# A new stored order for all pieces of an attention and feed-forward kernel

## The chip, the cores and the metric

One core of one Trainium2 chip runs the whole program. The metric is the device time of one execution in microseconds (us). Engines are named as in the profile: PE (TensorE), PEld (its weight loads), DVE (VectorE), ACT (ScalarE), POOL (GpSimd) and SP (SyncE, which only issues transfers). "Clock" is the share of full speed that PE was granted.

## The reference, cut to what matters

Forgetting attention over 8 batches and 8 heads of 576 rows by 64, then an RMS norm and a gated feed-forward part over the 4608 rows of 512:

```python
decay = cum[:, :, :, None] - cum[:, :, None, :]        # cum = cumsum(log f)
scores = where(causal, -1e9, scale * q @ k.T + decay)
attn = exp(scores - max); attn = attn / (sum(attn) + 1e-9)
x = (attn @ v)  # heads side by side: 4608 x 512
xn = x / sqrt(mean(x * x) + 1e-6) * rms_g              # 512 weights
g = xn @ w_gate; out = (g * sigmoid(g) * (xn @ w_val)) @ w_out      # 512 -> 1536 -> 512
```

Inputs and output are fp32; the kernel multiplies in bf16.

## The kernel before

The kernel is a list of some 1,500 pieces of work (load, cast, transpose, scores, exp, mask, values, norm, gate, projection, store). Each piece belongs to one engine, and each engine runs its own in order. A string, ORDER, gives the order of all of them; semaphores follow from what each piece reads and writes.

```python
ORDER = """
one lf ident Lk0.0 Lq0.1 rg identb clear Lk0.1 Lq0.0 ... clip turn_rg*48 ...     # *48: that many filler matmuls first
...
"""
```

Names that the argument needs: `L`, `C` and `Sv` load, cast and scale the inputs of a batch (`Ck3.0`: cast of k of batch 3, part 0; casts and scalings mostly on POOL), `msc` and `mask` apply the causal mask (POOL), `xn1.2` is the norm of block 2 of batch 1 (DVE), `xtr1.2` its transposes (PE), `pj`, `o` and `so` project a block, copy it out of PSUM and store it (PE, ACT, POOL), `g` and `v` are the gate and value matmuls.

```python
def norm(js, j):                                        # DVE, 40 times
    xn = T["xn", b, j] = xnp.tile([128, DM], BF16, name="xn", tag="xn")
    nc.vector.scalar_tensor_tensor(xn, in0=T["x", b][:, j, :], scalar=T["rs", b, js][:, j:j + 1], in1=rgb,
                                   op0=ALU.mult, op1=ALU.mult)
...
def store(j, c0, c1):                                   # the last group's from SP, all 32 others from POOL
    (nc.sync if end else nc.gpsimd).dma_start(out=out[t0 + j * 128:t0 + (j + 1) * 128, c0:c1],
                                              in_=T.pop(("o", g, j, c0))[:, 0:c1 - c0])
```

`rgb` is the RMS weight spread over all 128 partitions. Three `ores` buffers hold rows on their way out; a store gives its buffer back when it has landed.

The softmax here doesn't subtract the row's maximum and nothing guards it: scores larger than these inputs give would overflow.

Of the kernel before, what the change touches and what calls it, by code (L numbers as in the profile page):

```python
# [11 lines left out]
ACT = mybir.ActivationFunctionType  # L12
# [10 lines left out]
one lf ident Lk0.0 Lq0.1 rg identb clear Lk0.1 Lq0.0 Lq0.2 Lqk11 Lk0.2 clip turn_rg*48 keep_rgT Lqk00 Ck0.0 fetch_ln spread_rg*3 Lv0.0 Cq0.1 log scan  # L23
Lv0.1 Cq0.0 Ck0.1 tr0.01*29 tr0.00 Cq0.2 Lk0.3 keeptr0.00.k keeptr0.00.q keeptr0.01.k expo Lqk01 keeptr0.01.q tr0.02*7 sc0.1.0 keeptr0.02.q Lv0.40
esc0.1.0 twice keeptr0.02.k Lq0.3 Ck0.2 sc0.2.0*5 msc0.1.0 turn_dec esc0.2.0 Lv0.3 sc0.0.0 tr0.03 keep_rg msc0.2.0 keeptr0.03.k Lk1.0 keeptr0.03.q
Lv0.41 keep_dec sc0.3.0*8 wv0 tr0.10 esc0.3.0 Sv0.1 Lq1.0 wg1 esc0.0.0 Ck0.3 Lv1.40 Sv0.0 fetch msc0.0.0 Lv0.2 keeptr0.10.q val0.2.0*16 Lk1.2 xpo0.2.0
msc0.3.0 val0.0.0:ff*5 sc0.1.512 xpo0.0.0 val0.4.0 esc0.1.512 Cqk0 xpo0.4.0 val0.6.0:ff Cq0.3 xpo0.6.0 Lq1.2 Ck1.0 tr0.12*8 Lk1.1 sq0.1 sc0.0.512 wg0
Lq1.3 keeptr0.12.q keeptr0.10.k trt0 sq0.0 keeptrt0 sc0.3.512*1 esc0.3.512 ms0.0 rs0.0 keeptr0.12.k sc0.2.512*10 wv1 xn0.0 esc0.2.512 Sv0.3 wg2
sc0.1.1024*10 k4.0 xn0.1 Lq1.1 xtr0.0 esc0.1.1024 Lqk10 tri esc0.0.512 kxtr0.0 Lv1.41 xtr0.1*9 Sv0.2 sc0.2.1024 Cq1.0 kxtr0.1 sc4.0 Sv0.4 esc0.2.1024
Lk1.3 g0.0*1 msc0.1.1024 Lv1.0 sc0.0.1024 th0.0 v0.0f exp4.0 ga0.0 esc0.0.1024 sc0.0.384 g0.2 mask4.0 hga0.0 esc0.0.384 msc0.0.1024 sc0.1.384 tr1.0  # L30
esc0.1.384 sc0.2.384 wv2 val0.3.2 keeptr1.0.k keeptr1.0.q sc0.3.1024 th0.2 Cq1.2 val0.1.2:ff msc0.2.1024 esc0.2.384 v0.2f Lv1.2 xpo0.1.2 esc0.3.1024
xpo0.3.2 val0.0.2:ff ga0.2 val0.4.2 msc0.3.1024 sc0.3.384 xpo0.0.2 val0.2.2:ff esc0.3.384 wg3 hga0.2 sc1.0.0 esc1.0.0 xpo0.4.2 val0.5.2:ff Lv1.3 Cq1.1
val0.7.2:ff xpo0.2.2 val0.6.2 Cqk1 xpo0.7.2 xpo0.5.2 Ck1.2 trt1*2 g0.4 xpo0.6.2 Ck1.1 keeptrt1 sq0.3 Cq1.3 tr1.1 sq0.2 tr1.2 k4.1 keeptr1.1.q
keeptr1.1.k wv3 keeptr1.2.q sc4.1*2 sq0.4 Ck1.3 th0.4 ms0.2 tr1.3*8 Lv1.1 rs0.2 keeptr1.2.k ga0.4 esc1.0.512 wo0 xn0.3 v0.4f*4 xn0.2 keeptr1.3.k wo1
g0.6 exp4.1 Lk2.0 hga0.4 sc1.0.1024 keeptr1.3.q th0.6 xtr0.3 Lq2.3 v0.6f ga0.6 kxtr0.3 xn0.4 esc1.1.0 xtr0.2 Lqk20 g0.8 kxtr0.2 hga0.6 g1.0 th0.8
esc1.0.1024 ga0.8 v1.0f Sv1.0 Lk2.1 th1.0 sc1.1.512 ga1.0 g1.2 esc1.1.1024 Lq2.0 hga1.0 v0.8f th1.2 esc1.1.512 Lk2.3 ga1.2 g0.10 hga0.8 v1.2f
msc1.1.1024 th0.10 ga0.10 sc1.2.0 mask4.1 esc1.2.0 xtr0.4 g1.4 Sv1.4 kxtr0.4 hga1.2 esc1.2.512 v1.4f th1.4 msc1.0.1024 Lq2.1 v0.10f ga1.4 Sv1.2
sc1.2.1024 hga1.4 g1.6 esc1.3.0 hga0.10 Sv1.3 v1.6f th1.6 esc1.2.1024 ga1.6 g1.8 Lqk21 Sv1.1 v1.8f th1.8 ga1.8 sc1.3.512 esc1.3.512 val1.0.0 hga1.6
Lk2.2 val1.1.0:ff hga1.8 esc1.3.1024 g1.10 pj0.0.0 msc1.3.1024 th1.10 ga1.10 msc1.2.1024 Lv2.3 xpo1.1.0 Lv2.41 xpo1.0.0 val1.2.0:ff Ck2.0 val1.4.0:ff
xpo1.2.0 Lv3.41 pj0.0.0e Cq2.0 xpo1.4.0 val1.5.0 o0.0.0 val1.3.0:ff Ck2.1 Lq2.2 xpo1.5.0 val1.6.0:ff Ck2.3 Lk3.0 xpo1.3.0 tr2.0 Cq2.1 val1.7.0 Lqk31  # L40
xpo1.6.0 keeptr2.0.k Cqk2 tr2.1 Lk3.3 keeptr2.0.q pj0.1.0 Cq2.3 keeptr2.1.k Lq3.3 xpo1.7.0 keeptr2.1.q sq1.1 Lv2.40 Sv2.3 sq1.2 Lq3.0 pj0.1.0e so0.0.0
v1.10f o0.1.0 Ck2.2 Lq3.1 sq1.4 trt2 sc2.0.0 keeptrt2 sq1.0 Cq2.2 hga1.10 tr2.3 Lqk30 sq1.3 k4.2 tr2.2 pj1.0.0 Lv2.0 ms1.0 keeptr2.2.k keeptr2.2.q
rs1.0 esc2.0.512 keeptr2.3.q Lq3.2 keeptr2.3.k xn1.3 sc4.2 pj1.0.0e xn1.0 exp4.2 xtr1.3 o1.0.0 pj1.1.0 xn1.1 kxtr1.3 xn1.2 esc2.0.0 xn1.4 xtr1.0
xtr1.1 kxtr1.0 pj1.1.0e kxtr1.1 xtr1.2 sc2.0.1024 kxtr1.2 Cq3.0 esc2.0.1024 xtr1.4 g2.0 kxtr1.4 tq3.0 o1.1.0 Cq3.1 v2.0f th2.0 Cqk3 esc2.1.0 Lv2.1
ga2.0 g2.1 Cq3.3 tq3.1 hga2.0 Ck3.3 v2.1f th2.1 Ck3.0 ga2.1 sc2.1.512 Lv2.2 mask4.2 esc2.1.512 g2.2 hga2.1 Lq4.3 msc2.0.1024 v2.2f tk3.0 th2.2 Sv2.0
esc2.1.1024 ga2.2 g2.3 Lk4.0 hga2.2 Cq3.2 v2.3f th2.3 Lk3.1 Sv2.1 ga2.3 sc2.2.0 tt3 g2.4 esc2.2.512 hga2.3 Sv2.2 tq3.2 v2.4f th2.4 Sv2.4 esc2.2.0
ga2.4 g2.5 Lq4.1 v2.5f tq3.3 th2.5 msc2.1.1024 ga2.5 val2.1.0 sc2.2.1024 Ck3.1 hga2.4 esc2.2.1024 g2.6 xpo2.1.0 Lk3.2 hga2.5 v2.6f msc2.2.1024 th2.6
tk3.1 esc2.3.0 ga2.6 val2.0.0 k4.3 val2.2.0:ff tk3.3 hga2.6 sc2.3.512 xpo2.2.0 g2.7 esc2.3.1024 xpo2.0.0 Lv3.3 val2.4.0:ff th2.7 Lqk40 sc4.3 v2.7f
xpo2.4.0 esc2.3.512 Lv3.2 ga2.7 val2.5.0 exp4.3 Lv3.0 msc2.3.1024 g2.8 hga2.7 Lv3.40 xpo2.5.0 sc3.0.0 mask4.3 Lq4.0 esc3.0.0 val2.6.0:ff Ck3.2
val2.3.0 xpo2.6.0 Cq4.3 tk3.2 th2.8 v2.8f Ck4.0 xpo2.3.0 g2.9 ga2.8 val2.7.0 hga2.8 th2.9 v2.9f Sv3.2 xpo2.7.0 esc3.0.512 tq4.3 ga2.9 g2.10 sq2.4  # L50
Sv3.3 hga2.9 v2.10f Lv3.1 sq2.3 so1.1.0 th2.10 tk4.0 g2.11 sq2.1 Sv3.0 ga2.10 sc3.0.1024 sq2.0 Lqk41 hga2.10 v2.11f Sv3.4 th2.11 Lk4.3 sq2.2 ga2.11
pj2.0.0 Lk4.1 esc3.0.1024 ms2.0 hga2.11 Cq4.0 esc3.1.0 so0.1.0 tq4.0 rs2.0 pj2.0.0e sc3.1.512 o2.0.0 Lk4.2 msc3.0.1024 pj2.1.0 xn2.1 esc3.1.1024
esc3.1.512 xn2.0 tx2.1.3 xn2.4 pj2.1.0e sc3.2.0 xn2.2 esc3.2.0 Lv4.3 pj2.2.0 Ck4.1 Lv5.41 esc3.2.512 so2.0.0 tx2.0.3 Sv3.1 pj2.2.0e tx2.2.3 sc3.2.1024
so1.0.0 esc3.2.1024 pj2.3.0 msc3.1.1024 Lq4.2 o2.1.0 esc3.3.0 Cq4.1 Lv5.40 Ck4.3 Lqk51 o2.2.0 val3.1.0 msc3.2.1024 Lk5.3 val3.3.0:ff xpo3.1.0
val3.0.0:ff tk4.1 Cqk4 sc3.3.512 xpo3.0.0 val3.5.0 esc3.3.1024 xpo3.3.0 pj2.3.0e val3.2.0:ff Cq4.2 xpo3.5.0 o2.3.0 g3.0 esc3.3.512 xpo3.2.0 tq4.1
v3.0f xn2.3 th3.0 msc3.3.1024 g3.1 ga3.0 Lq5.3 val3.4.0 so2.3.0 tk4.3 hga3.0 th3.1 v3.1f Ck4.2 ga3.1 Ck5.3 val3.7.0:ff tq4.2 xpo3.4.0 g3.2 xpo3.7.0
val3.6.0 hga3.1 Lqk50 th3.2 v3.2f Lv4.0 ga3.2 g3.3 Lk5.0 xpo3.6.0 hga3.2 tx2.4.4 v3.3f th3.3 sq3.2 ga3.3 g3.4 tt4 hga3.3 v3.4f th3.4 Sv4.0 sq3.1 Lq5.2
ga3.4 sc4.0.0 g3.5 Lq5.0 esc4.0.512 hga3.4 Lq5.1 v3.5f th3.5 Lv4.1 sq3.4 ga3.5 g3.6 k4.4 esc4.0.0 tk4.2 hga3.5 Ck5.0 v3.6f th3.6 Sv5.4 g3.7 ga3.6
sc4.2.0 th3.7 hga3.6 so2.2.0 v3.7f sq3.3 ga3.7 Sv4.3 tk5.0 esc4.2.512 g3.8 hga3.7 Cqk5 v3.8f th3.8 tx2.3.4 sq3.0 ga3.8 sc4.4 g3.9 esc4.2.0 Lv4.41
hga3.8 v3.9f Lk5.2 ms3.0 exp4.4 th3.9 mask4.4 sc4.0.1024 Lv4.40 esc4.0.1024 ga3.9 g3.10 Sv4.1 Lv4.2 hga3.9 esc4.1.0 v3.10f Cq5.0 g3.11 th3.10 rs3.0  # L60
tq5.0 ga3.10 sc4.1.512 Cq5.3 esc4.1.512 v3.11f hga3.10 Lv5.0 so2.1.0 xn3.0 tt5 th3.11 pj3.0.0 Cq5.2 ga3.11 Sv4.4 Lq6.3 hga3.11 Lqk71 xn3.1 pj3.0.0e
Lk5.1 Sv4.2 pj3.1.0 o3.0.0 xn3.2 tx3.0.4 esc4.1.1024 so3.0.0 Ck5.2 tx3.2.4 pj3.1.0e pj3.2.0 msc4.1.1024 tx3.1.4 Lv5.1 pj3.2.0e sc4.2.1024 o3.2.0 Lv6.1
val4.2.0 esc4.2.1024 tq5.2 pj3.3.0 xpo4.2.0 esc4.3.0 msc4.2.1024 o3.1.0 Ck5.1 Lq6.0 val4.3.0 msc4.0.1024 pj3.3.0e Lv5.3 xpo4.3.0 g4.0 o3.3.0 k4.5
Lv6.41 xn3.3 sc4.3.512 th4.0 Sv5.1 tq5.3 val4.4.0 esc4.3.1024 ga4.0 v4.0f xpo4.4.0 tk5.3 val4.5.0:ff Cq5.1 hga4.0 g4.1 so3.2.0 xpo4.5.0 tq5.1 Sv5.0
val4.1.0 th4.1 v4.1f ga4.1 Cq6.3 g4.2 so3.1.0 hga4.1 tk5.1 Sv5.3 v4.2f xpo4.1.0 th4.2 esc4.3.512 ga4.2 tk5.2 sc4.5 g4.3 so3.3.0 exp4.5 hga4.2
msc4.3.1024 v4.3f th4.3 Lqk61 ga4.3 g4.4 Lq6.2 hga4.3 Lqk60 val4.0.0 th4.4 val4.6.0:ff tx3.2.5 xpo4.0.0 v4.4f ga4.4 sc5.0.0 Lk6.1 xpo4.6.0 esc5.0.0
g4.5 hga4.4 Lq6.1 esc5.0.512 v4.5f Lk6.0 Cqk6 g4.6 th4.5 tt6 ga4.5 sc5.0.1024 th4.6 v4.6f esc5.1.0 ga4.6 Lq7.0 val4.7.0 hga4.5 tx3.3.5 g4.7 hga4.6
xpo4.7.0 v4.7f th4.7 Lv5.2 Ck6.0 sq4.3 ga4.7 Cq6.0 g4.8 tk6.0 esc5.0.1024 xn3.4 v4.8f hga4.7 th4.8 msc5.0.1024 sc5.1.512 sq4.0 Lv7.1 ga4.8 g4.9 Lk6.2
# [108 lines left out]
def kernel(  # L177
# [16 lines left out]
    def pool(name, bufs, **kw):  # L194
# [10 lines left out]
    plan = Plan({"st": N_ST, "ld": N_LD, "pt": N_PT, "x": 2, "xn": N_XN, "xT": 3, "hT": 2, "th": 3, "ga": 2,  # L205
                 "ores": 3, "sc": 2, "po": 1, "ff": 3})
# [705 lines left out]
```

## Time and profile before

| | before |
|---|---|
| time, median of 4 runs | 383.8 us (383.36 to 384.61) |
| span of the profiled run, mean clock | 382.2 us, 0.995 |
| PE busy | 366.8 us, 96% |
| POOL busy | 171.5 us, 45% |
| the 40 norms on DVE, summed one by one | 35.1 us, the longest 1.83 us |

PE is the bound nearly everywhere, so idle PE is what an order can change: length of a window less PE busy in it.

```profile
L688 DVE SCALAR_TENSOR_TENSOR xn<-x,rs,rgb 128x512 bf16<-128x512 f32 x40 | 33.9, 877 | 5.4 <-POOL rs L684 5.3
```

A line of the groups view has busy us of the group, mean ns of one, idle time before them and what ended it. Forty norms at a mean of 877 ns; alone, one takes 740 to 750.

### The profile page before, as it was taken

The page shows a single profiled execution, that of the slowest core. Times are in us where ns is not written, and L with a number is a line of the kernel's source. Part 1 is how long each engine was busy: PE and PEld are TensorE (multiplying, and loading weights), DVE is VectorE, ACT ScalarE, POOL GpSimd, SP SyncE. Part 2 cuts the span into 40 slices and gives each one's busy share as a digit, 9 for nine tenths or more (in the row PEclk, how much of TensorE's full clock was granted, in tenths as well). Part 3 has the DMA queues.
Part 4 walks back from the last instruction along what each step waited for, and adds up shares of the span by engine and source line. Part 5 has one row for each costly group of instructions (what it writes and reads, how often), then busy time and mean ns, then how long its engine had stood idle before and what let it go on. Part 6 is the DMA issues. An engine that isn't in the chain of part 4 may idle for free.

```text
span 382.2 us, 8426 instructions
## 1 busy us (share of the span) xinstructions
PE 366.8 (96%) x3270; PEld 203.7 (53%) x3314; DVE 243.5 (64%) x460; ACT 215.1 (56%) x357; POOL 171.5 (45%) x281
## 2 busy tenths in 40 slices
PE   8768899989999999999999999999999999999996
PEld 8646787744554644454445544554444544444443
DVE  4676875776774776467855877487348845743750
ACT  2676786578687568356655496556554353313322
POOL 4485626878397546792673359224111221001000
PEclk9899999999999999999999999999999999999999
DMA  8999996799859998999987964830001224022002
GB/s 204 212 262 234 228 234 143 166 210 175 175 118 241 188 182 177 206 198 164 219 176 133 200 149 100 119 106 14 14 30 21 84 69 98 1 63 83 0 5 108
DMA packets 144840, 52.62 MB, mean 138 GB/s; under 512 B 128220, under 2 KB 142304, under 8 KB 144800
## 3 DMA queue, kind: packets, MB, share of 16 engines
q1 hardware_dynamic: 136336, 38.82, 52.8%
q0 software_dynamic: 8384, 13.11, 14.9%
q8 instruction: 26, 0.43, 0.5%
q14 instruction: 14, 0.11, 0.1%
q10 hardware_dynamic: 80, 0.15, 0.1%
HBM read 37.90 MB, written 9.44 MB: 124 GB/s over the span
## 4 chain that ended last, share of the span: by engine, by line
PE 88%; DVE 3%; ACT 3%; DMA 2%; issue 1%; POOL 1%; POOLq 0%; ACTq 0%
PE ff L811 49%; PE ff L837 23%; PE sc L620 6%; PE po L656 4%; PE ff L656 3%; DMA wg<-in_moe_w_gate_dram 2%; PE ff L235 2%; DVE xn L688 1%; ACT junk L673 1%; DVE x L666 1%; POOL PT L636 1%; ACT QK L513 1%; DVE QK L513 1%; PE ff L491 0%; ACT L271 0%
## 5 line engine op out<-in xcount | busy, mean ns | idle before, releaser
L820 DVE SCALAR_TENSOR_TENSOR ga<-th,ff 128x512 f32<-128x512 f32 x108 | 74.2, 687 | 67.6 <-ACT th L816 66.0
L628 ACT ACTIVATE PT<-sc 128x1024 bf16<-128x1024 f32 (+2 forms) x100 | 96.8, 990 | 28.4 <-PE sc L620 28.3
L811 PE MATMUL ff<-xT,wg 128*128 128x512 bf16 (+1 forms) x467 | 110.2, 357 | 1.9 <-DMA wg<-in_moe_w_gate_dram 1.0
L811 PE MATMUL ff<-xT,wv 128*128 128x512 bf16 (+1 forms) x464 | 109.7, 357 | 0.8
L816 ACT ACTIVATE th<-ff 128x512 f32<-128x512 f32 x108 | 64.5, 597 | 73.4 <-PE ff L811 68.2
L837 PE MATMUL ff<-wo,hT 128*128 128x512 bf16 (+1 forms) x429 | 97.2, 373 | 0.7
L827 DVE SCALAR_TENSOR_TENSOR hT<-ga,ff 128x512 bf16<-128x512 f32 x108 | 73.8, 686 | 7.9 <-PE ff L811 0.2
L636 POOL TENSOR_SCALAR_AFFINE_SELECT PT<-PT 128x1024 bf16<-128x1024 bf16 (+1 forms) x44 | 37.2, 856 | 77.1 <-ACT PT L628 75.7
L811 PEld LDWEIGHTS <-wg 128*128 128x128 bf16 x480 | 44.7, 98 | 44.3 <-issue 1.7
L811 PEld LDWEIGHTS <-wv 128*128 128x128 bf16 x480 | 45.1, 98 | 42.4 <-issue 1.0
L837 PEld LDWEIGHTS <-hT 128*128 128x128 bf16 x444 | 42.2, 98 | 46.4 <-issue 1.1
L412 POOL CAST ld<-st 128x512 bf16<-128x512 f32 x68 | 42.7, 651 | 23.6 <-DMA st<-in_q_dram 9.8
L842 ACT COPY ores<-ff 128x512 f32<-128x512 f32 (+1 forms) x37 | 21.1, 575 | 48.5 <-PE ff L837 41.4
L656 PEld LDWEIGHTS <-PT 128*128 128x128 bf16 x896 | 33.6, 98 | 10.7 <-issue 1.3
L688 DVE SCALAR_TENSOR_TENSOR xn<-x,rs,rgb 128x512 bf16<-128x512 f32 x40 | 33.9, 877 | 5.4 <-POOL rs L684 5.3
L845 POOL DMA_DIRECT2D out_dram<-ores x32 | 18.4, 576 | 39.6 <-ACT ores L842 39.6
L419 POOL TENSOR_TENSOR Vs<-st,decT 128x512 bf16<-128x512 f32 x27 | 29.1, 1078 | 8.9 <-DMA st<-in_v_dram 8.5
L620 PE MATMUL sc<-QK 64*128 64x128 bf16 (+2 forms) x328 | 29.2, 273 | 1.1 <-DVE QK L508 1.0
L673 ACT ACTIVATE junk<-x 128x512 bf16<-128x512 f32 x40 | 25.1, 628 | 3.0 <-DVE x L666 2.5
L620 PEld LDWEIGHTS <-QK 64*128 64x128 bf16 x584 | 16.0, 95 | 18.3 <-issue 13.3
L656 PE MATMUL po<-Vs,PT 128*128 128x65 bf16 x521 | 22.3, 194 | 0.2 <-DVE Vs L420 0.2
L666 DVE TENSOR_TENSOR x<-po,rden 128x320 f32<-128x320 f32 (+2 forms) x39 | 18.6, 478 | 1.3
(84 smaller groups left out, 231.5 us busy)
## 6 DMA issues: line engine op xcount, KB each, us to landing
st<-in_k_dram SPq DMA_DIRECT2D x32, 256.0 KB, 4.9
st<-in_q_dram SPq DMA_DIRECT2D x32, 256.0 KB, 4.5
st<-in_v_dram SPq DMA_DIRECT2D x32, 256.0 KB, 4.3
out_dram<-ores POOLq DMA_DIRECT2D x32, 256.0 KB, 3.0
wo<-in_moe_w_out_dram POOLq DMA_DIRECT2D x2, 768.0 KB, 13.9
st<-in_k_dram SPq DMA_DIRECT2D x8, 128.0 KB, 4.8
st<-in_q_dram SPq DMA_DIRECT2D x8, 128.0 KB, 5.1
st<-in_v_dram SPq DMA_DIRECT2D x16, 64.0 KB, 4.3
```

The costliest lines, as they stand in the source:

```text
L412: {"DVE": nc.vector.tensor_copy, "POOL": nc.gpsimd.tensor_copy, "ACT": nc.scalar.copy}[eng](o, x)
L419: e.tensor_tensor(Vs[i][:, j, :, 0:D], t, bcast(dj, D), ALU.mult)
L620: nc.tensor.matmul(sc[:, par, c:c + n], lhsT=k_cols(r, p, kj), rhs=q_cols(r, p, q0, n), start=True, stop=True)
L628: nc.scalar.activation(T["pt", b, p][:, :, c0:c0 + n], T.pop(("sc", b, p, c0))[:, :, 0:n], ACT.Exp, scale=scale)
L636: nc.gpsimd.affine_select(out=d, in_=d, pattern=[[0, m], [1, 128]], compare_op=ALU.is_ge, fill=0.0, base=0, channel_multiplier=-1)
L656: nc.tensor.matmul(T["po", b, hs][:, qm, m, :], lhsT=w, rhs=Vs[i][:, kj, h, :], start=(kj == 0), stop=(kj == qi))
L688: nc.vector.scalar_tensor_tensor(xn, in0=T["x", b][:, j, :], scalar=T["rs", b, js][:, j:j + 1], in1=rgb, op0=ALU.mult, op1=ALU.mult)
L811: nc.tensor.matmul(ps[:, c * w:c * w + w], lhsT=wt[:, dc, (fc + c) * 128:(fc + c + 1) * 128], rhs=T["xT", g][:, dc, 0:w], start=(dc == 0), ...
L816: nc.scalar.activation(t, T["pg", g, fc], ACT.Tanh, scale=0.5)
L820: nc.vector.scalar_tensor_tensor(a, in0=T.pop(("th", g, fc)), scalar=1.0, in1=T.pop(("pg", g, fc)), op0=ALU.add, op1=ALU.mult)
L827: nc.vector.scalar_tensor_tensor(o, in0=T.pop(("ga", g, fc)).rearrange("p (c t) -> p c t", t=w), scalar=0.5, in1=T.pop(("pv", g, fc)).rear ...
L837: nc.tensor.matmul(po, lhsT=T["hT", g][:, fc, j * 128:(j + 1) * 128], rhs=wo[:, fc, c0:c1], start=(fc == 0), stop=(fc == NFC - 1))
```

## The change

Its intent: fetch the exp table ahead of the decay, load q, k and v of batch 0 before those of batch 1, and group score visits on PE. Engines, pools and pieces stay. Apart from ORDER two lines add a dependency on the table fetch for the planner.

```diff
-    p_exp = plan.add("expo", "ACT", 0.78, expo, [p_scan])
+    p_exp = plan.add("expo", "ACT", 0.78, expo, [p_scan, p_pre])
 ...   # the same for every exp of scores
-one lf ident Lk0.0 Lq0.1 rg identb clear Lk0.1 Lq0.0 Lq0.2 Lqk11 Lk0.2 clip turn_rg*48 ... log scan ... expo ... fetch ...
+one lf ident Lk1.0 clear Lq0.1 fetch_ln tri Lq0.0 Lk0.1 identb Lk0.2 Lk0.0 clip ... log ... scan fetch ... tr0.02*48 ... expo ...
 ...   # around the norms of batch 1:
-... xn1.3 sc4.2 pj1.0.0e xn1.0 exp4.2 xtr1.3 o1.0.0 pj1.1.0 xn1.1 kxtr1.3 xn1.2 esc2.0.0 xn1.4 xtr1.0 ... Cq3.0 ...
+... xn1.4 Cq3.3 tk3.0 tr2.3 xtr1.1 xn1.3 keeptr2.3.k pj1.1.0 so0.1.0 esc2.0.1024 xn1.2 mask4.2 kxtr1.1 ... Sv2.1 xtr1.2 ...
 ...   # and some 1,500 more words in another order
```

## The prediction

> **What bounds the kernel now.** I read the page's first two parts first: which engine is full, and in which slices of the span it isn't.
>
> ```profile
> PE 366.8 (96%) x3270; PEld 203.7 (53%) x3314; DVE 243.5 (64%) x460; ACT 215.1 (56%) x357; POOL 171.5 (45%) x281
> ...
> PE   8768899989999999999999999999999999999996
> ...
> PEclk9899999999999999999999999999999999999999
> DMA  8999996799859998999987964830001224022002
> ```
>
> PE is full from the fourth slice (each is 9.6 us) to the last but one; no other engine comes near. A new order of the same pieces can't shorten full slices, only the head and the last slice. To size those I cut the span by hand into windows of busy time:
>
> ```profile
> 0.00:31.00 31.00, 23.55 (x304) 19.33 (x306) 18.61 (x51) 17.08 (x27) 17.78 (x39) 0.94 1.10 227
> 31.00:46.00 15.00, 13.86 (x236) 11.31 (x232) 11.25 (x30) 11.13 (x23) 10.86 (x20) 1.00 1.20 230
> 46.00:86.00 40.00, 38.79 (x470) 28.23 (x472) 29.12 (x56) 27.34 (x46) 24.66 (x39) 1.00 0.94 190
> 86.00:340.00 254.00, 251.94 (x2084) 126.19 (x2119) 168.02 (x300) 147.67 (x244) 116.05 (x181) 1.00 0.65 126
> 340.00:382.20 42.20, 38.67 (x189) 18.62 (x190) 16.50 (x24) 11.91 (x21) 2.15 (x4) 0.99 0.17 57
> ```
>
> Length less PE busy (second column of numbers) is idle PE: 7.5, 1.1, 1.2, 2.1 and 3.5 us. But busy PE is not yet useful PE: the kernel multiplies a zero tile by itself (tile `idle`, the `*n` in the order) where it expects to wait, to keep the clock up. The PE timeline up to 46 us gives them:
>
> ```profile
> 1.09 5.14 PE L235 MATMUL ff<-idle 128*128 128x128 bf16 x48 [1.09 <-DVE idle L245]
> ...
> 16.47 1.06 PE L235 MATMUL po<-idle 128*128 128x128 bf16 x16
> ...
> 23.34 0.72 PE L235 MATMUL sc<-idle 128*128 128x128 bf16 x10 [1.29 <-ACT PT L628]
> ...
> 29.88 1.05 PE L811 MATMUL ff<-xT,wg 128*128 128x256 bf16 x8 [0.97 <-DMA wg<-in_moe_w_gate_dram]
> ```
>
> Such rows up to 31 us add up to 14.0 us, from 31 to 46 us to 1.6 us. So PE time without use, idle plus filler, is **21.5 us up to 31 us, 2.7 us up to 46, 1.2 up to 86, 2.1 over the next 254 us, 3.5 in the tail**: 31 us of 382. The last row is the first gate matmul of the feed-forward part (g0.0), at 29.88 us: from there PE always has work at hand. **When g0.0 can start, and how much attention is done by then, is the case.** What g0.0 waited for:
>
> ```profile
> PE sc L235 <- ACT PT L628: 2.4, 2, 1.3
> ...
> PE ff L811 <- DMA wg<-in_moe_w_gate_dram: 1.0, 1, 1.0
> ```
>
> 2.4 us for exps to free score buffers, and at last 1.0 us for the gate weights.
>
> **What the Trainium skill says.** "TensorE: Matmul & The Clock Gate", Part 1 (The HAM clock gate): the clock starts at half rate and drops back after about 3.4 us of low activity. The trace agrees: the first 48 fillers took 107 ns each, later ones 53 to 56, and the clock record shows half rate once more from 12.8 to 16.2 us. "ScalarE: Activation LUTs", What ACT_TABLE_LOAD costs: about 1283 ns for a load plus a drain of about 1380 when the function set changes. The load agrees (1.28 us at 1.39 us and again at 10.06 us, before the exp of the decay); no separate drain of that length shows. "DMA: Bandwidth & Descriptors", Issuing engines are not separate DMA queues: all queues share the same 16 DMA engines. This agrees: weights issued on POOL stretched the q/k/v loads on SP, whose landings were 1.0 to 1.4 us apart mostly, but 2.7 us apart around 21.5 us.
>
> **The change, part by part.** Two lines only add dependencies: `expo` and every exp now follow `fetch`. The pools, engines and instructions stay, only ORDER is new.
>
> 1. *Steady PE work.* From 46 us on I matched PE's weight loads to the pieces of the order. A gate of 4 wide matmuls takes 0.86 us, a head's values 0.58 to 0.64, a two-bank score visit 0.55. What costs extra is going over to scores: a gate followed by scores takes 1.17 us instead of 0.86. I counted the neighbours in both orders: scores follow scores 3 times in each, and changes between kinds are 238 before, 237 after. "Grouped" visits therefore save nothing countable: **0 us**.
>
> 2. *Exp table.* Before, log ended at 5.9 us, and the table came at 10.06 us, in ACT's way; after, `fetch` stands right after log, so the 1.28 us lies beside the scan (5.9 to 8.4 us). But `expo` now stands behind two score exps in ACT's queue: first scores 9.9 us (below), exps until about 13.2, decay exp until 14.0, decay transposed and copied by 16.5 us. Before it was copied by 15.8. So the decay is not earlier. But no value could start then anyway: see 3.
>
> 3. *Loads.* SP's order puts k of batch 1 first, then q/k of batch 0 of both halves, and v0.0 and v0.1 as loads 12 and 13 (tails as halves), not 8 and 9. In the trace load 4 landed at 7.5 us, load 6 or so at 10.0, load 13 at about 18.3. So heads 4 to 7 have q/k at 7.7, are cast by 8.3, transposed, copied by 9.75 and scored from 9.9 us (before: 11.0); heads 0 to 3 wait for k0.0 until 10.0, and are turned at 10.8 us (before 8.9). v0.1 lands at 18.3 to 19, its scaling (0.87 us in DVE's queue) ends at 19.6, and the first values start at 19.7 instead of 17.3: **2.4 us later**.
>
> 4. *From values to g0.0.* Before: last values 19.1, g0.0 possible at 29.0 but held by the weights to 29.88. The 10 us are mostly ACT: it had exps of 0.93 us each ahead of the squares and the last copy of xT. After, ACT's row is, from 20.6 us: two short exps and the tail exp (0.9), two long (1.9, to 23.1), two squares (1.4, to 24.5), copy of rg (0.5); power on POOL and two norms to 27.1; three long exps (2.8, to 27.8), then the copy of xT: 28.3. Its weights wg0 are now issued first of all, at about 15.4, not 20.7, so the 1.0 us wait goes. I put **g0.0 at 29.3**, with a us for waits that I don't see.
>
> 5. *What is done by then.* Useful PE time before g0.0 was 7.6 us. In the new order four more score banks (0.45, 0.45, 0.2, 0.2) and two transposes of batch 1 (0.84) stand ahead of it, one bank (0.45) behind: 9.3 us. Lost time at g0.0: 29.88 - 7.6 = 22.3 before, 29.3 - 9.3 = 20.0 after: **2.3 us gained**.
>
> 6. *31 to 46 us.* Before, 2.7 us went around the transposes of batch 1. After, they still wait: q/k 3 and 2 of batch 1 are loads 20 to 23 of SP, landing near 36 to 40 us, and v0.4f needs a weight piece that landed at 41.3 before. Fillers here are 14 instead of 16. I take **0**.
>
> 7. *Rest.* At 79 to 84 us PE lost about 1 us waiting for the normed x of batch 1; the new order puts a score visit and transposes in between: **0.3 us gained**. In the middle, the stretch from a pair's last scores to its values falls to 3 to 4 us of PE work in places (4.8 at least before), where score, exp and mask take 2.6 to 2.8 at best: I charge 0.6 us. The last group's 48 projections and their store are the same words: 0.
>
> Sum: 0 + 0 + 2.3 + 0 + 0.3 - 0.6 = 2.0 us less: **382.2 us**.
>
> **Rivals.** *The later values win:* v lands late, and all of the 2.4 us reaches g0.0, since norm and transposes hang on it; for it speaks that ACT idled 14 of 31 us, against it that ACT gets through score exps meanwhile. That gives 384 to 387 us. *The clock:* the fillers are 126 instead of 176, and from 6.2 to 8.4 us PE has nothing; were it at half rate until 20 us, each of about six pieces on the chain doubles (0.2 us each), +1 us; at g0.0, where 3.4 us of slow gates would cost 1.7 us, PE is about two thirds busy before and should be warm. *DMA is the bound of the whole head:* at 227 to 230 GB/s up to 46 us the same bytes must land before the third gate group whatever the order, and everything gained is given back at v0.4f; that gives 384. *Early scores pay more:* with nine of twelve late banks scored before g0.0, PE doesn't pause at 39 to 46: 379.5.
>
> **Range and chances.** All rivals move it by 2 to 5 us; 2% are 7.7 us, a third of what is lost in the head. Range **379.2 to 386.0**; faster by over 2% **0.04**, within 2% **0.93**, slower **0.03**.
>
> **What would show it.** Right: first values near 19.7 us, g0.0 near 29 with no wait for wg, idle plus filler up to g0.0 about 20 us, 46 to 340 us within 1 us of before, the tail equal. Wrong: g0.0 after 31 us, half clock beyond 20 us, waits for wg or wv over 1 us after 37 us, or new waits for masks (PT from POOL) in the middle.

## The result, and the profile after

| | before | after |
|---|---|---|
| time, median of 4 runs | 383.8 us | **395.35 us** (394.28 to 396.2) |
| ratio | | **1.0297**, 95% interval 1.0265 to 1.0329 |
| span and clock of the profiled run | 382.2 us, 0.995 | 393.6 us, 0.974 |
| the 40 norms, summed one by one | 35.1 us | 47.5 us |

A ratio here is the mean time of one kernel's runs over that of the other's of the same rounds, so it is not quite the ratio of the medians that I quote.

The change made the kernel 3% slower. The page of the kernel after, parts 1 and 2:

```profile
PE 369.7 (94%) x3220; PEld 203.7 (52%) x3264; DVE 254.7 (65%) x460; ACT 216.4 (55%) x357; POOL 174.1 (44%) x281
...
PE   6879999849999899999999999999999999999996
...
PEclk9688999996999999999999999999999999999999
```

Slices are 9.8 us here. Two dips in PE are new: the ninth slice (79 to 89 us) at 4 and, slightly, the fourteenth; and the clock dips to 0.6 in the tenth (89 to 98 us). The same windows as the prediction's (window and its length, then busy us of PE, PEld, DVE, ACT and POOL, then clock, DMA share and GB/s):

```profile
0.00:31.00 31.00, 24.18 (x272) 18.48 (x273) 18.93 (x49) 18.90 (x31) 22.20 (x44) 0.82 1.10 224
31.00:46.00 15.00, 14.04 (x228) 11.52 (x227) 12.68 (x33) 11.22 (x22) 9.54 (x17) 0.92 1.24 211
46.00:86.00 40.00, 36.36 (x438) 26.88 (x439) 30.09 (x52) 25.64 (x42) 26.11 (x42) 1.00 0.90 182
86.00:340.00 254.00, 245.11 (x2049) 123.10 (x2086) 168.23 (x293) 145.72 (x239) 114.08 (x177) 0.99 0.68 130
340.00:393.60 53.60, 50.05 (x241) 23.73 (x243) 24.74 (x36) 14.89 (x26) 2.15 (x4) 1.00 0.11 40
```

Idle PE is 6.8, 1.0, 3.6, 8.9 and 3.6 us, where it was 7.5, 1.1, 1.2, 2.1 and 3.5. The head, which the change was about, has no more idle time; the 9.3 us of new idle time lie in the third and fourth rows. What PE waited for (us in total, times, longest):

```profile
PE ff L716 <- DVE QK L514: 5.0, 1, 5.0
...
PE ff L838 <- DVE x L667: 1.8, 1, 1.8
```

One wait of 5.0 us leads; before, the longest was 1.3. Line 716 is the transpose of normed rows, and the PE timeline puts the wait at batch 1 (start, duration, then in brackets the idle time before and who ended it):

```profile
81.35 2.32 PE L838 MATMUL ff<-wo,hT 128*128 128x512 bf16 x10
88.70 0.59 PE L716 MATMUL ff<-ident,xn 128*128 128x128 bf16 x4 [5.04 <-DVE QK L514]
```

The view names DVE's copy of QK, which came last. That copy had only queued behind something. DVE's timeline, and the source view of the norms' line from 78 to 89 us (shortest, median and longest in ns):

```profile
80.56 7.49 DVE L689 SCALAR_TENSOR_TENSOR xn<-x,rs,rgb 128x512 bf16<-128x512 f32 x3
87.97 0.68 DVE L514 COPY QK<-ff 128x512 bf16<-128x512 bf16 x1
```

```profile
L689 DVE SCALAR_TENSOR_TENSOR xn<-x,rs,rgb x5: 742/1092/5808, 78.1 to 82.2; 128x512 bf16<-128x512 f32 x5
```

**A norm that takes 0.74 us alone took 5.81 us.** It is `xn1.2`, started at 82.24 us. For the same five norms the kernel before has:

```profile
L688 DVE SCALAR_TENSOR_TENSOR xn<-x,rs,rgb x5: 740/1091/1182, 78.8 to 82.6; 128x512 bf16<-128x512 f32 x5
```

Nothing that the norm needs was late: it had begun. So I looked at who else was at work, POOL, in the kernel after:

```profile
78.07 3.71 POOL L413 CAST ld<-st 128x512 bf16<-128x512 f32 x4
81.72 0.66 POOL L846 DMA_DIRECT2D out_dram<-ores  x1
82.41 0.68 POOL L598 TENSOR_TENSOR P<-P,tri 128x256 bf16<-128x256 bf16 x1
83.04 1.05 POOL L420 TENSOR_TENSOR Vs<-st,decT 128x512 bf16<-128x512 f32 x1
84.02 0.22 POOL L421 CAST Vs<-decT 128x8 bf16<-128x8 f32 x1
...
86.35 1.16 POOL L413 CAST ld<-st 128x512 bf16<-128x512 f32 x2
87.48 1.47 POOL L420 TENSOR_TENSOR Vs<-st,decT 128x512 bf16<-128x512 f32 x1
```

The norm started 0.14 us before POOL had issued a store (81.72 + 0.66 = 82.38). Behind the issue POOL had work for many us without a pause. Eight of its instructions ran to their end at their usual lengths; only the ninth, at 87.48, was slowed: this multiply took 1.47 instead of its usual 1.05, and the norm ended at 88.05. The Trainium skill offers the tie between the two: "SBUF — State Buffer", Who interferes with whom, says that a DVE instruction with two SBUF inputs takes its second through a read port that GpSimd uses too; the same page, SBUF: two separate sides, that whichever starts first keeps it for its whole instruction, and that the other is blocked. It does not say that the blocked one can miss eight turns.

Two more norms suffered so. The second of batch 2, started at 126.13 us, 0.37 us before an issue ended, took 5.92 us; the fourth of batch 3, at 176.18, 0.25 us before an issue ended, took 2.42 us. In the kernel before, the worst norm (1.83 us, at 235.59) had started 0.03 us before the end of an issue.

**Where the 11.4 us of span are (an estimate).** I laid PE's weight loads along each order and took from the elapsed time each piece's usual time. That gives PE time lost up to a piece:

| lost up to | before | after | difference |
|---|---|---|---|
| g1.6 (starts at 59.4 before, 56.2 after) | 25.5 | 24.7 | -0.8 |
| g2.6 (batch 1's norms in between) | 27.6 | 35.3 | +7.7 |
| g3.0 (batch 2's) | 28.5 | 39.2 | +10.7 |
| g4.6 (batch 3's) | 29.8 | 41.3 | +11.5 |
| end | 32.1 | 43.5 | +11.4 |

The head gained 0.8; the stretches of the three starved norms lost 8.5, 3.0 and 0.8. Redone from the start times of these gates alone, with the few pieces that only one order has before them, they come to about 8, 3 and 1, so the table is good to half a us or so. The 8.5 are more than the one wait of 5.0: PE's clock fell to half from 87.95 to 94.77 us right after it, which costs at most half of that, 3.4 us.

### The profile page after: what moved, and what is told of

The parts are those of the page before. It is cut to its first block, busy times and chain, and to the rows that moved or that the text cites. A ratio compares the mean times of both kernels' runs of the same rounds, so it can differ in the third digit from the quotient of the medians. Undisturbed runs are those within 1.5% of the kernel's fastest.

```text
span 393.6 us, 8327 instructions
## 1 busy us (share of the span) xinstructions
PE 369.7 (94%) x3220; PEld 203.7 (52%) x3264; DVE 254.7 (65%) x460; ACT 216.4 (55%) x357; POOL 174.1 (44%) x281
## 3 DMA queue, kind: packets, MB, share of 16 engines
HBM read 37.90 MB, written 9.44 MB: 120 GB/s over the span
## 4 chain that ended last, share of the span: by engine, by line
PE 76%; DVE 9%; POOL 6%; issue 3%; DMA 3%; ACT 2%; SPq 0%; POOLq 0%; ACTq 0%
PE ff L812 45%; PE ff L838 19%; DVE xn L689 6%; PE sc L621 5%; PE po L657 4%; POOL ld L413 2%; DVE x L667 1%; POOL Vs L420 1%; PE ff L657 1%; DMA xT<-xn 1%; DMA st<-in_q_dram 1%; DMA st<-in_v_dram 1%; POOL rs L685 1%; POOL PT L637 1%; PE ff L716 1%
## 5 line engine op out<-in xcount | busy, mean ns | idle before, releaser
L812 PE MATMUL ff<-xT,wg 128*128 128x512 bf16 (+1 forms) x467 | 111.5, 362 | 1.9 <-DMA xT<-xn 0.9
L629 ACT ACTIVATE PT<-sc 128x1024 bf16<-128x1024 f32 (+2 forms) x100 | 96.4, 991 | 28.5 <-PE sc L621 26.9
L812 PEld LDWEIGHTS <-wv 128*128 128x128 bf16 x480 | 44.8, 98 | 43.5 <-issue 3.4
L637 POOL TENSOR_SCALAR_AFFINE_SELECT PT<-PT 128x1024 bf16<-128x1024 bf16 (+1 forms) x44 | 38.2, 882 | 64.9 <-ACT PT L629 62.1
L689 DVE SCALAR_TENSOR_TENSOR xn<-x,rs,rgb 128x512 bf16<-128x512 f32 x40 | 46.2, 1186 | 5.6 <-POOL rs L685 5.5
L846 POOL DMA_DIRECT2D out_dram<-ores x32 | 18.5, 578 | 42.8 <-ACT ores L843 42.8
L621 PE MATMUL sc<-QK 64*128 64x128 bf16 (+2 forms) x328 | 30.0, 280 | 1.0 <-DVE QK L509 0.7
L685 POOL TENSOR_TENSOR rs<-ms,mhalf 128x5 f32<-128x5 f32 (+2 forms) x9 | 10.0, 1111 | 37.7 <-DVE ms L680 33.5
L657 PE MATMUL po<-Vs,PT 128*128 128x65 bf16 x557 | 23.9, 194 | 0.6 <-DVE Vs L421 0.6
```

The lines of the kernel that those rows point to most:

```text
L621: nc.tensor.matmul(sc[:, par, c:c + n], lhsT=k_cols(r, p, kj), rhs=q_cols(r, p, q0, n), start=True, stop=True)
L629: nc.scalar.activation(T["pt", b, p][:, :, c0:c0 + n], T.pop(("sc", b, p, c0))[:, :, 0:n], ACT.Exp, scale=scale)
L637: nc.gpsimd.affine_select(out=d, in_=d, pattern=[[0, m], [1, 128]], compare_op=ALU.is_ge, fill=0.0, base=0, channel_multiplier=-1)
L657: nc.tensor.matmul(T["po", b, hs][:, qm, m, :], lhsT=w, rhs=Vs[i][:, kj, h, :], start=(kj == 0), stop=(kj == qi))
L812: nc.tensor.matmul(ps[:, c * w:c * w + w], lhsT=wt[:, dc, (fc + c) * 128:(fc + c + 1) * 128], rhs=T["xT", g][:, dc, 0:w], start=(dc == 0), ...
```

## The experiments

**Theory A:** a norm that starts in the last few tenths of a us of a POOL store issue loses its turn to the row of POOL work behind it, and the three such norms are the whole loss. Runs 1 to 4 were made for its first form, a row of POOL work alone; the store came into it after run 4, and "the last 0.4 us" only with run 9. **Rivals:** the order of PE pieces itself (grouped score visits, later values) costs the time and the norms only happen to be late; or any full row of POOL work starves a norm, store or not; or DMA of the later loads. All runs are compared with the kernel before; that was 382.79 us for runs 1 to 4, 383.22 for 5 to 8, 383.7 for 9 and 10 and 384.06 for the last two. Kernels are compared only within the same rounds.

### 1. Norm with one SBUF input (wrong result on purpose)

```diff
# on the kernel after
-nc.vector.scalar_tensor_tensor(xn, in0=x, scalar=rs, in1=rgb, op0=ALU.mult, op1=ALU.mult)
+nc.vector.tensor_scalar(xn, in0=x, scalar1=rs, op0=ALU.mult, scalar2=0.0, op1=ALU.add, accum_out=waste)
```

> The kernel after, same order, but each of the 40 norms reads one SBUF tensor instead of two (x times its rstd, without the rms weight; the result is wrong on purpose) and also writes a sum, so that it should keep its 0.75 us form. Theory (the norms of batches 1, 2 and 3 starve behind a row of POOL instructions because their second SBUF input goes over a port that they share with POOL): all 40 norms near 0.75 to 0.9 us, none over 1.2; the 5.0 us wait of PE at the transposes of batch 1 and the half clock at 88 to 95 us are gone; time 383 to 386 us. Rival 1 (the new order of transposes, projections and score visits on PE itself is at fault, or loads that come late): norms may be short, but PE still waits there and the time stays at 393 to 396.

The RMS weight is left out, so the output is wrong (relative error 0.68). **381.65 us (380.47 to 382.57), ratio 0.9957 (0.9924 to 0.999).** The norms' line of the groups view:

```profile
L689 DVE TENSOR_SCALAR_CACHE_REDUCE xn<-x,rs 128x512 bf16<-128x512 f32 x40 | 28.4, 741 | 5.6 <-POOL rs L685 5.5
```

All 40 took 730 to 750 ns wherever they started, some of them within a store issue, and the 5.0 us wait is gone. The order of PE, the loads and the stores are those of the slow kernel. So the order of PE pieces costs nothing that shows; the norm's second SBUF input does. (The time is below the 383 to 386 us that I had expected.)

### 2 and 3. A hold on POOL until the norm is done

A tiny POOL copy that reads the norm's output, put ahead of the row of work, makes POOL wait for the norm. It takes nothing away and stays free of races.

```diff
# on the kernel after; run 2: the first hold alone
+plan.add("hold1", "POOL", 0.1, lambda: nc.gpsimd.tensor_copy(scrap[:, n:n + 1], T["xn", 1, 2][:, 0:1]))
-... xn1.2 mask4.2 ...
+... xn1.2 hold1 mask4.2 ...
# run 3: also for batches 2 and 3
-... xn2.1 tx2.0.3 mask4.3 ... xn2.4 sc3.2.0 Ck4.3 ... xn2.2 ...        ... xn3.4 Ck5.3 ...
+... xn2.1 tx2.0.3 ...        xn2.4 sc3.2.0 ...        xn2.2 hold2 mask4.3 Ck4.3 ...   ... xn3.4 hold3 Ck5.3 ...
```

> The kernel after plus one small POOL copy that reads the last norm of batch 1, queued before the mask of the tail of batch 2, so that POOL pauses until that norm is done. All else as after. Theory: this norm falls from 5.8 us to about 1 us, the 5.0 us wait and the half clock after it go, 7 to 8 us less: 387 to 389 us; the starved norm of batch 2 (5.9 us) stays. Rival 1 (order of PE, late loads): 394 to 396, since POOL only comes later. Rival 2 (POOL's work itself is late and on the path): slower than after.

One hold: **384.59 us (381.9 to 387.16), ratio 1.0035 (0.997 to 1.0099)**. The norm took 0.74 us; the second of batch 2 now took 4.36 and the one of batch 3 still 2.43. I had expected less of it; the runs spread over 5 us, and I can't say why one hold brings nearly as much as three.

> The kernel after plus three such pauses of POOL: before the tail mask of batch 2 (as in e2), before the tail mask of batch 3 and a cast of k of batch 4 (both moved behind the first four norms of batch 2), before a cast of k of batch 5 (behind the fourth norm of batch 3). Theory: the three starved norms fall to about 1 us each; the gain of e2 plus 3 us in batch 2 and 0.9 in batch 3: 383 to 385.5 us, the level of before. Rival 1: 394 to 396. If only 387 to 389, the loss in batches 2 and 3 has another cause.

Three holds: **382.92 us (382.43 to 383.08), ratio 0.9988 (0.9956 to 1.0019)**. No norm took over 1.67 us, all 40 sum to 35.0 us as before, and the windows' PE idle time from 46 to 340 us fell from 12.5 to 1.7 us. The two later windows:

```profile
46.00:86.00 40.00, 38.83 (x467) 28.11 (x462) 27.30 (x55) 26.66 (x46) 26.34 (x43) 1.00 0.92 191
86.00:340.00 254.00, 253.46 (x2107) 125.35 (x2105) 166.23 (x301) 147.32 (x241) 113.76 (x178) 1.00 0.62 129
```

So three norms hold the whole gap.

### 4. The row of POOL work pulled in, in the kernel before (a miss)

```diff
# on the kernel before
-... xn1.1 kxtr1.3 xn1.2 ...            ... mask4.2 ... Sv2.0 ...
+... xn1.1 mask4.2 Sv2.0 kxtr1.3 xn1.2 ...
```

> The kernel before with two POOL pieces (tail mask of batch 2, scaling of v block 0 of batch 2) pulled ahead among the norms of batch 1, as the kernel after has them. PE's, ACT's and DVE's order unchanged. Theory: one of the later norms of batch 1 is starved for the length of the POOL row, 2 to 5 us, PE waits about as long at a transpose of batch 1: 385.5 to 390 us. Rival 1 (PE's order): 383.5 to 384.5, as before. If POOL and DVE take turns instead (each norm 1.1 us), also 384: then a row of POOL work is not enough and something else decides who gets the port.

**382.96 us (382.7 to 383.42), ratio 0.9994 (0.9968 to 1.0021).** Batch 1's norms took 0.74 to 1.16 us: POOL had pauses, since `Sv2.0` waited for its load until 82.74 us. No row without a pause arose, so nothing is learnt of such a row; POOL work beside norms alone is not enough. By the expectation's own terms something else had to decide, and this is where the store came in.

### 5. The three stores later, nothing else (in the kernel after)

```diff
-... pj1.1.0 so0.1.0 esc2.0.1024 xn1.2 ...    ... esc3.1.512 so2.0.0 xn2.1 ...    ... xpo4.2.0 so3.2.0 v4.0f ...
+... Sv2.2 so0.1.0 ...                        ... msc3.1.1024 so2.0.0 ...         ... Sv5.2 so3.2.0 ...
```

> The kernel after with nothing added; only three output stores, whose DMA POOL issues, are moved behind the rows of POOL work that starved a norm (in after each of these stores was issued just as the starved norm began). Theory A (a norm that begins while POOL issues a DMA loses its turn to the whole row that follows; one that begins inside a POOL compute instruction waits for that one only): the three norms take at most 1.5 us each, time 382 to 385.5 us, though POOL's rows are as long as before. Theory B (a long gapless row of POOL work is enough): still norms of 2 to 6 us and 390 to 396 us.

**388.68 us (388.5 to 388.77), ratio 1.0131 (1.0097 to 1.0164).** The norms answer to theory A: POOL's rows of work are as long as in the slow kernel, but no norm took over 1.67 us. The time does not: a new wait took the old one's place.

```profile
PE ff L812 <- ACT ores L843: 4.0, 1, 4.0
```

The late store keeps its `ores` buffer, ACT's next copy waits for it, PE waits for ACT, and the clock is at half from 89.88 to 93.29 us. I had not asked what a later store holds.

### 6. A gap within the row (in the kernel after)

```diff
-... mask4.2 kxtr1.1 keeptr2.3.q esc2.1.0 Sv2.1 xtr1.2 ...
+... mask4.2 kxtr1.1 keeptr2.3.q esc2.1.0 Sv2.1 hold1 xtr1.2 ...
```

> The kernel after plus one POOL copy that reads the last norm of batch 1, queued not before the row of POOL work but inside it, after the tail mask and one scaling of v (ending 2.0 us after the norm began in after). Theory: the norm stays blocked until POOL stops there, so it takes 2.5 to 2.8 us (5.8 in after, 0.74 with the pause ahead of the row), PE's wait falls from 5.0 to about 2 us, 384.5 to 388 us with the starved norms of batches 2 and 3 left as they are. If the norm takes about 1.1 us, it was not the row that blocked it.

**388.13 us (387.29 to 389.51), ratio 1.012 (1.008 to 1.0161).** The norm took 2.40 us, close to the 2.5 to 2.8 expected: it finished beside the last instruction before the hold, so here the loss ended with the row. PE waits for it 1.6 us now, not 5.0; the starved norms of batches 2 and 3 stay, at 4.36 and 2.45 (5.92 and 2.42 in the kernel after).

### 7. One store moved into a row of casts (in the kernel before)

```diff
# on the kernel before
-... pj0.1.0e so0.0.0 v1.10f ...       ... Cq3.1 v2.0f ...
+... pj0.1.0e v1.10f ...               ... Cq3.1 so0.0.0 v2.0f ...
```

> The kernel before with one output store (POOL issues it) moved from 73 us to between the casts that POOL does during the norms of batch 1. Theory A: the norm that begins within that issue is starved behind the four casts left and the mask, 2 to 4 us instead of 1.1; PE waits 1 to 3 us more at a transpose of batch 1: 384 to 387 us. If the norm begins too early or too late by chance, 383 and no norm above 1.2 us, and the run says nothing.

**389.31 us (386.68 to 390.65), ratio 1.0127 (1.0066 to 1.0189).** POOL of this kernel, the norms' source view, and PE's first wait:

```profile
83.55 0.66 POOL L845 DMA_DIRECT2D out_dram<-ores  x1
84.21 2.28 POOL L412 CAST ld<-st 128x512 bf16<-128x512 f32 x4
86.46 0.66 POOL L597 TENSOR_TENSOR P<-P,tri 128x256 bf16<-128x256 bf16 x1
```

```profile
L688 DVE SCALAR_TENSOR_TENSOR xn<-x,rs,rgb x5: 739/1093/3617, 81.3 to 87.6; 128x512 bf16<-128x512 f32 x5
```

```profile
PE ff L715 <- DVE xT L722: 2.8, 1, 2.8
```

The norm at 84.06 us, 0.15 before the issue's end, waited out all four casts and the mask. In the kernel before the same casts took turns with the norms. **Moving one 0.66 us store brings the starved norm into the fast order.** The time missed the 384 to 387 expected, and part of the 6 us is other things: these norms began 2.5 us later than in the kernel before (81.28 against 78.81); this run's head was at half clock twice, for 3.4 us each, and waited 1.8 us for the gate weights (1.0 in the prediction's profile). After the wait of 2.8 us the clock fell to half again, from 90.12 to 93.53.

### 8. Three holds and a warm head (in the kernel after)

The order of run 3 with 72 more filler matmuls in the head:

```diff
-tr0.02*48 ... tr0.10*12 ... tr1.0 ... xtr0.1*2
+tr0.02*82 ... tr0.10*24 ... tr1.0*20 ... xtr0.1*8
```

> The kernel of e3 with 72 more filler matmuls at four places of the head where PE has nothing to do (before the first transposes, before the transposes of the second half, before the first transposes of batch 1, before the second of x). They should keep the full clock where after and e3 fell to half from 7 to 14 or 9 to 16 us and for 3.4 to 6.8 us around 25 to 33 us. Clock theory: 1 to 2 us less than e3's 382.9, 381 to 382 us, clock 0.99 or more. If the chain of loads and exps sets the head whatever PE's clock: 382.5 to 383.5. If the fillers delay real work: above 383.5.

**382.76 us (381.84 to 383.78), ratio 0.9978 (0.9936 to 1.0019)**, at a clock of 1.00 throughout the profiled run. That is run 3's 382.92 within the spread: the half clock in the head is not what holds the changed order back by any amount that shows here.

### 9 and 10. All stores issued by SP

```diff
-(nc.sync if end else nc.gpsimd).dma_start(out=..., in_=...)
+nc.sync.dma_start(out=..., in_=...)
-plan.add("s" + ko, *(("SP", 0.45) if end else ("POOL", 0.6)), ...)
+plan.add("s" + ko, "SP", 0.45, ...)
```

> The changed kernel with all 32 output stores issued by SP instead of POOL, nothing else. Theory A (a norm that starts in the last 0.4 us of a POOL store issue misses its turn for the whole row of POOL work behind it): no norm can start within a store issue any more, so no norm over about 1.7 us, sum of the 40 norms near 35 us as in before, no 5 us wait at batch 1's transposes, and 382 to 385 us. POOL is freed of some 32 issues of 0.6 us besides, which should be worth little as POOL is busy under half of the span. Rival B (SP is in order: a store waits there for ACT's copy, and the loads and transposes behind it on SP are issued late): new waits of PE for DMA xT or x, and 386 us or more. Rival C (the starving does not need a store issue, any full row of POOL work does it): norms of 2.4 us and more remain.

On the kernel after: **384.47 us (383.27 to 386.51), ratio 1.0024 (0.9991 to 1.0057).** No store issue is left on POOL, and from 75 to 90 us the norms are back to:

```profile
L689 DVE SCALAR_TENSOR_TENSOR xn<-x,rs,rgb x5: 741/1091/1152, 76.6 to 80.7; 128x512 bf16<-128x512 f32 x5
```

POOL's row behind them is as full as in the slow kernel, and DVE and POOL take turns. The longest of all 40 took 1.57 us, their sum is 37.4. Two lines of code, with no new order, take back 2.7 of the 3.0%. The rival "any full row starves" falls for this order. The rival "stores on SP hold up the loads" does not show: PE's longest waits are 1.5 us or less.

> The kernel before with all 32 output stores issued by SP instead of POOL. Theory A: its one norm of 1.83 us goes, the time gains at most a microsecond: 381 to 384 us. Rival B (stores hold up the loads behind them on SP): slower, 385 us or more, with PE waits for DMA xT or x.

On the kernel before: **383.76 us (381.99 to 386.77), ratio 1.0006 (0.9966 to 1.0046)**. Nothing to gain there, as that order had met only one such norm.

### 11 and 12. A correct one-input norm (a miss)

Run 1 was the fastest of all, with a wrong result. To make it correct, the RMS weight can be multiplied into the gate and value weights once:

```diff
+for c in range(NDC):                    # for each of the 8 weight loads, on DVE, in place
+    nc.vector.tensor_scalar(w[:, c, c0:c1], in0=w[:, c, c0:c1], scalar1=rgT[:, c:c + 1], op0=ALU.mult, scalar2=None)
-spread_rg, keep_rg                      # 4 transposes and a copy that made rgb
 # and the norm of run 1
```

> The changed kernel made correct with a one-input norm: the RMS weight is multiplied into the gate and value weights once, by 32 small DVE instructions in place (four for each of the eight weight loads), and the spreading of the weight over all rows (4 PE transposes, 1 ACT copy) goes; the norm is the accumulating form x times rs as in the first experiment. Theory A: all 40 norms 0.73 to 0.75 us wherever they start, as the first experiment showed (0.9957 of before with a wrong result). The 32 small ones should take about 0.2 us each, some 6 us of DVE between 25 and 48 us, of which part fits DVE's idle stretches (2 us before the first norm, 1 us before ga0.0); the rest may delay the first FFN steps. Expected 381 to 384.5 us, middle 382.5. Rival: the head is bound by DVE here and gives back more than the norms saved: 385 us or more, with PE waits for DVE's ga or for the folded weights before 50 us.

On the kernel after: **389.61 us (388.48 to 390.34), ratio 1.0139 (1.011 to 1.0169)**, correct. The norms are at 740 ns as in run 1, but the 32 multiplications took 11.1 us where I had estimated 6:

```profile
L354 DVE TENSOR_SCALAR wv<-wv,rgT 128x256 bf16<-128x256 bf16 (+1 forms) x16 | 6.0, 458 | 0.3 <-DMA wv<-in_moe_w_val_dram 0.3
L354 DVE TENSOR_SCALAR wg<-wg,rgT 128x256 bf16<-128x256 bf16 (+1 forms) x16 | 5.1, 403 | 0.7 <-DMA wg<-in_moe_w_gate_dram 0.7
```

They fall between 25 and 56 us, where DVE has no such room. Against run 1, idle PE is 0.9 us more up to 31 us, 1.2 up to 46, 3.1 up to 86 and 2.5 up to 340: 7.7 us, about the 8.0 between the two medians. Which piece of DVE's work each of these waits hangs on I have not followed.

> The kernel before with the same edit. Theory A: its norms took 35.1 us in all, little above 40 times 0.75, so at most 2 us are to be had; expected 381 to 384.5 us, within 1% of before. Rival: as for the other kernel, 385 us or more with DVE waits before 50 us.

On the kernel before: **391.41 us (389.21 to 392.57), ratio 1.0175 (1.0135 to 1.0214)**, for the same kind of reason: PE waited 2.6 us for DVE's `x` and 2.1 for its copy of `xT`. The rival told in advance, that the head has no DVE time to give, is what happened. No correct version that I ran beats the kernel before by more than the noise.

### What the runs say together

Norms that started within a POOL *computation* took at most 1.58 us in all these traces, however long the row behind: they waited for that one instruction, and then the two took turns. Norms that started in the last 0.4 us (0.03 to 0.38) of a POOL *store issue* with at least four POOL instructions following without a pause mostly took 1.7 to 5.9 us: 5.81, 5.92 and 2.42 in the kernel after, 1.83 before, 4.36 and 2.43 in run 2, 2.40, 4.36 and 2.45 in run 6, 3.62 in run 7, besides some of 1.67 and 1.84; one behind a weight load's issue took 1.30. Norms with over 0.5 us of the issue still to come took 0.74 to 1.22 us. Nor is the row always missed as a whole: the norm of 2.42 us missed two instructions of a row of four and ran beside the third, the one of 1.83 missed two and ran beside the next store's issue, and the norm that took 5.92 us by missing seven took 4.36 in run 2, with the same row behind it, by missing four. There are counter-cases: in the kernel before, and again in runs 4 and 7, the first norm of batch 3 started 0.2 us before the end of an issue with ten instructions behind it and took 0.81 us; and in runs 7 and 10 the second norm of batch 0 started 0.1 us before the end of a weight load's issue and took 0.75. So all norms of over 1.6 us had started there, yet starting there isn't always enough; what else decides, and how many turns are missed, is open.

## Why the prediction was wrong, point by point

- **Step 1, steady PE work, 0 us: held.** Run 1 shows that the new order of PE pieces costs nothing that can be seen.
- **Step 2, exp table, and step 3, loads: held.** First scores were at 9.51 us (9.9 predicted) and v0.1 landed at 18.43 (18.3). The first two value matmuls ran at 18.87 us, the others from 19.69 on (19.7), after a wait of 0.60 us for the scaled v; in the kernel before they began at 17.70, where the prediction read 17.3.
- **Steps 4 and 5, g0.0 at 29.3 and 2.3 us gained: right in kind, too large.** There was no wait for gate weights. But g0.0 came at 31.28, at half clock:

```profile
25.17 0.62 PE L492 MATMUL ff<-ident,ld 128*128 128x128 bf16 x8 [1.49 <-DVE ms L680]
...
31.28 1.91 PE L812 MATMUL ff<-xT,wg 128*128 128x256 bf16 x8
```

  PE waited 1.49 us at the transposes of batch 1, whose q parts landed at 23.63 and 24.45 us and had then to be cast, and the clock was at half from 26.5 to 33.3 us: the eight gate matmuls took 1.91 us instead of 1.05. "PE should be warm" was wrong. At g0.6 (46 us) the order was about 0.4 us ahead, not 2.3: it started 0.1 us later, with one score visit of some 0.55 us more done. The clock alone isn't the reason: in run 8, at full clock throughout, g0.0 came at 31.43. Why it was no earlier there stays open.
- **Step 6, 31 to 46 us, 0: held.** Idle PE there is 1.0 us, as before 1.1.
- **Step 7, the rest, 0.3 gained and 0.6 charged: this step failed.** It put the middle within about 1 us of before; the stretches of the norms of batches 1 to 3 lost some 8.5, 3.0 and 0.8 us, because three norms took 5.81, 5.92 and 2.42 us and not about 0.75 to 1.2. I had looked at those very norms ("PE lost about 1 us waiting for the normed x of batch 1") and counted the PE work between scores and values, but took every DVE and POOL instruction to last what it lasted before. A new order changes durations as well: which instructions overlap decides who waits for the shared port. I read the skill's pages on the clock, the tables and DMA, and not the one on SBUF, though the norm has two SBUF inputs and stands beside POOL.
- **The rivals.** Later values, clock, DMA and early scores: none of them is what made the kernel slower. The clock did fall to half in the head, from 9.44 to 16.27 and from 26.51 to 33.33 us, but run 8 without that is no faster than run 3. That an engine's instruction might be starved by another engine's was missing altogether, and so the chance of "slower" was set at 0.03.
- **What would show it.** "46 to 340 us within 1 us of before" is the line that failed: 12.5 us idle against 3.3. The tail is equal, as said (3.6 and 3.5 us). Two of its signs of being wrong came true, g0.0 after 31 us and half clock beyond 20 us, but they belong to the head, not to the loss. Idle plus filler up to g0.0 was 6.8 + 11.6 = 18.5 us, less than the 20 foretold, yet other matmuls ran at half clock; by the count of step 5 the time lost at g0.0 was 31.28 - 9.3 = 22.0, not 20.0.
- **Numbers read loosely.** 2.0 us less is 382.2 only from 384.2, the median of the three runs known then; from 383.8 it is 381.8. The landings on SP up to 25 us were mostly 0.7 to 1.4 us apart, not 1.0 to 1.4. Neither bears on the loss.

## What to carry to other kernels

When a list of instructions is reordered, durations are not constants: look at what each DVE instruction with two SBUF inputs will now run beside on POOL. Keep transfers off the queue of an engine that computes in long rows beside such instructions; here, issuing the stores from SP made a bad order harmless (1.0024 of before), in two lines. And when a wait names an engine, ask whether the instruction it names was late to start or long in running: the 5.0 us were put down to a copy that only stood behind a norm of 5.8 us.

## What the Trainium skill lacked or had wrong

- "SBUF — State Buffer", Who interferes with whom: the two-input rule agrees (two-input norms 0.74 to 5.92 us beside POOL, the accumulating one-input form 0.73 to 0.75 us everywhere), but the page lets the second comer wait for one instruction. The runs show a norm that missed eight in a row (5.81 us); when it began within a POOL computation it waited for one (up to 1.58 us), when it began at the end of a POOL store issue it mostly missed one to eight.
- The same page warns of DVE, in its two-port modes, holding up transfers that POOL issues. No page that I read has the reverse: a store issue on POOL, 0.58 us each in both kernels, that costs a DVE instruction its turn afterwards (3.62 us with the store moved in, at most 1.18 for those five norms without).
- What decides between 0.81 us and 5.9 us for a norm that starts at the end of an issue no page says, and these runs don't settle it.
